# Group-dependent start addresses for the gated values and for w_in in a Fourier filter with a gated feed-forward

## The chip, the cores and the metric

The kernel runs on one core of a Trainium2 chip. The metric is the device time of one execution in microseconds; every number below is in microseconds (us) unless it says ns. The engines are named as in the profile: PE (TensorE, the matmuls), PEld (the loading of the stationary operand of a matmul, the "weights"), DVE (VectorE), ACT (ScalarE), POOL (GpSimd) and SP (SyncE, which issues the DMAs).

## The reference

Input x is 8 batches of 3136 rows by 256 columns. It is filtered along the rows in the Fourier domain, and the result goes through a feed-forward with an inner width of 1024:

```python
X = np.fft.rfft(x, axis=1)
x = np.fft.irfft(X * (filt_r + 1j * filt_i)[None], n=3136, axis=1).astype(np.float32)
h = np.maximum(x @ w_in, 0.0)                       # w_in 256 x 1024
conv = sum(conv_w[k] * shift(h, k - 1) for k in range(3))   # along the rows, per column
gate = 1.0 / (1.0 + np.exp(-conv))
out = (h * gate @ w_out).astype(np.float32)         # w_out 1024 x 256
```

## The kernel before

There are two stages. The forward stage transforms, filters and transforms back with matmuls by table (`first`, `second`, `filt`, `third`), with an intermediate in DRAM between them; w_in and w_out arrive in it as doubles, are turned to float32 by DVE, and are then split into a high and a low part (`convert_weights`: ACT writes the high part, POOL the low part, `hi_act` and `lo_pool`). `wi[0]`, `wi[1]` are the high and the low part of w_in, `wo[0]`, `wo[1]` those of w_out.

The second stage is the feed-forward. It runs over `j` (28 pieces of 896 rows), within that over `f` (8 groups of 128 of the inner width) and within that over `i` (2 halves of 448 rows). A step `m` is one (j, f, i). The order on every engine is written out by hand (`tc.manual_schedule`): in round m PE does `inner` of step m, in some rounds the last part of the inverse transform of the next batch (`last_stage`, 8 matmul instructions on line L216), and `project` of step m - 6. The other engines follow behind: `relu` and `conv` of step m - 1, `gate` of step m - 2, `split_g` of step m - 3.

Every product is made of three matmuls, high by high, high by low, low by high:

- `inner(j, f, i)`: 6 matmuls (lines L177, L178, L179 for each of two halves k of the 256 columns). The stationary operand is 128 columns of `wi[0]` or `wi[1]`, the moving operand 450 columns of `ys[b][0]` or `ys[b][1]`, the high and low part of the filtered rows (`y0`, `y1` below).
- `project(j, f, i)`: for 4 or 3 blocks of 128 rows, 3 matmuls each (lines L475, L476, L477). The stationary operand is 128 columns of the gated values `g0` (high) or `g1` (low), the moving operand 256 columns of `wo[0]` or `wo[1]`.

So the stationary operand of one matmul is read from SBUF while the moving operand of the matmul before it streams, and both reads go to fixed addresses. In the program's layout all of those addresses are the same modulo 256 bytes, whatever the group, the half, the batch and the buffer:

| operand | bytes between its slices | start modulo 256 |
|---|---|---|
| `wi[0]`, `wi[1]` of group f (stationary) | 512 per f, 4096 per k | 160 |
| `y0`, k = 0 and k = 1 (moving) | 1792 per half of rows | 160, 168 |
| `y1`, k = 0 and k = 1 (moving) | 1792 per half of rows | 192, 200 |
| `g0`, `g1` (stationary), four buffers each | 512 per block, 3584 per buffer | 224 |
| `wo[0]`, `wo[1]` of group f (moving) | 1024 per f | 160 |
| `br`, loaded for L216 (stationary) | 512 | 160 |
| `t`, from which `g0` and `g1` are made | 1792 per buffer | 224 |

`br` is what `last_stage` loads as its stationary operand.

Of the kernel before, what the change touches and what calls it, by code (L numbers as in the profile page):

```python
# [10 lines left out]
F32R = mybir.dt.float32r  # L11
# [10 lines left out]
FF = 1024  # L22
KT = D // 128
NF = FF // 128
SUB = 448
NSUB = S // SUB
CH = 2 * SUB
NT = CH // 128


def _k1(g, s):
# [93 lines left out]
def tile_fft_filter_gated_ffn(  # L125
# [19 lines left out]
    def hi_act(dst, src):  # L145
        nc.scalar.activation(dst, src, AF.Copy)  # L146
# [4 lines left out]
    def lo_pool(dst, src, hi):  # L151
        nc.gpsimd.tensor_tensor(out=dst, in0=src, in1=hi.bitcast(F32), op=ALU.subtract)  # L152

    def to_f32(dst, raw, e, m):


        v = nc.vector
        pairs = raw.rearrange("p (n t) -> p n t", t=2)
        low, high = pairs[:, :, 0].bitcast(U32), pairs[:, :, 1]
        v.tensor_scalar(e, high, 3, 0x3FFFFFF8, op0=ALU.logical_shift_left, op1=ALU.bitwise_and)  # L160
        yield
        v.tensor_scalar(m, high, 30, 30, op0=ALU.logical_shift_right, op1=ALU.logical_shift_left)
        yield
        v.tensor_tensor(out=e, in0=e, in1=m, op=ALU.bitwise_or)
        yield
        v.tensor_scalar(m, high, 27, 0xF, op0=ALU.logical_shift_right, op1=ALU.bitwise_and)
        yield
        v.scalar_tensor_tensor(out=dst, in0=m, scalar=7.0, in1=e.bitcast(F32), op0=ALU.is_ge, op1=ALU.mult)
        yield
        v.tensor_scalar(e, dst.bitcast(I32), 23, 23, op0=ALU.logical_shift_right, op1=ALU.logical_shift_left)  # L170
        yield
        v.scalar_tensor_tensor(out=e.bitcast(F32), in0=low, scalar=2.0**-52, in1=e.bitcast(F32), op0=ALU.mult, op1=ALU.mult)
        yield
        nc.gpsimd.tensor_tensor(out=dst, in0=dst, in1=e.bitcast(F32), op=ALU.add)

    def mm3(ps, wh, wl, rh, rl, start=True, stop=True, **kw):
        nc.tensor.matmul(ps, lhsT=wh, rhs=rh, start=start, stop=False, **kw)  # L177
        nc.tensor.matmul(ps, lhsT=wh, rhs=rl, start=False, stop=False, **kw)  # L178
        nc.tensor.matmul(ps, lhsT=wl, rhs=rh, start=False, stop=stop, **kw)  # L179
# [5 lines left out]
    wc = ctx.enter_context(tc.tile_pool(name="wc", bufs=1))  # L185
# [1 line left out]
    cw = wc.tile([128, 3, NF], F32, name="cw")  # L187
    nc.gpsimd.memset(cw[:, 0, 0:1], 0.0)
    nc.scalar.activation(cw[:, 0, 0:1], cw[:, 0, 0:1], AF.Sigmoid)
    wi = [wc.tile([128, KT, FF], F32R, name=f"wi{h}") for h in range(2)]  # L190
    wo = [wc.tile([128, NF, D], F32R, name=f"wo{h}") for h in range(2)]


    ys, yps = {}, []
# [33 lines left out]
    with (  # L228
# [31 lines left out]
        def load_weights(k):  # L260
            raws[k] = raw = cv.tile([128, 2, 512], I32, name="raw")
            for part, src in enumerate((w_in, w_out)):
                nc.sync.dma_start(out=raw[:, part], in_=src[:, 512 * k:512 * k + 512])
# [9 lines left out]
        def convert_weights():  # L273

            for k in range(8):
                raw = raws.pop(k)
                em = cv.tile([128, 2, 512], I32, name="em", bufs=1)
                ws = cv.tile([128, 2, 256], F32, name="ws")
                yield from to_f32(ws.rearrange("p t n -> p (t n)"), raw.rearrange("p t n -> p (t n)"), em[:, 0], em[:, 1])
                yield  # L280
                parts = [[t.rearrange("p a b -> p (a b)")[:, 256 * k:256 * k + 256] for t in w] for w in (wi, wo)]
                for part, (wh, wl) in enumerate(parts):
                    hi_act(wh, ws[:, part])
                yield
                for part, (wh, wl) in enumerate(parts):
                    lo_pool(wl, ws[:, part], wh)
                    yield
                if k < 6:
                    load_weights(k + 2)

        NP = 14
        parts = {}
# [68 lines left out]
        for c in range(1, 4):  # L361
            nc.sync.dma_start(out=s1_sb[:, 4 * c:4 * c + 4], in_=s1[:, 4 * c:4 * c + 4])
            load("x", 0, 2 * c)
            load("x", 0, 2 * c + 1)
        csteps, wsteps = convert_conv(), convert_weights()
        done = NP * B + 8
        NI = max(NP * B + SKEW + 5, done + N2 // 2 + 3)
        with tc.manual_schedule(engines=COMPUTE):
            for i in range(NI):
                f, m = i, i - SKEW  # L370
# [16 lines left out]
                if 12 <= i < 26 and i % 2 == 0:  # L387
                    sl = slice((i - 12) // 2 * 4, (i - 12) // 2 * 4 + 4)
# [31 lines left out]
    wp = ctx.enter_context(tc.tile_pool(name="wp", bufs=2, reuse_waits="tile"))  # L420
    ps_h = ctx.enter_context(tc.tile_pool(name="ps_h", bufs=4, space=bass.MemoryType.PSUM, reuse_waits="tile"))
    ps_o = ctx.enter_context(tc.tile_pool(name="ps_o", bufs=1, space=bass.MemoryType.PSUM, reuse_waits="tile"))

    outv = out.rearrange("b s d -> (b s) d").rearrange("(j t p) d -> j p t d", p=128, t=NT)
    hs, ts, gs, pos = {}, {}, {}, {}
# [4 lines left out]

    def inner(j, f, i):
        ps = ps_h.tile([128, 512], F32, name="ps_h")[:, 0:SUB + 2]
        fs = slice(128 * f, 128 * f + 128)
        b, u = divmod(2 * j + i, NSUB)
        us = slice(u * SUB, u * SUB + SUB + 2)
        for k in range(KT):
            mm3(ps, wi[0][:, k, fs], wi[1][:, k, fs], ys[b][0][:, k, us], ys[b][1][:, k, us], start=k == 0, stop=k == KT - 1)
        hs[j, f, i] = ps

    def relu(j, f, i):  # L440
# [16 lines left out]
    def split_g(j, f, i):  # L457
        t = ts.pop((j, f, i))
        if i == 0:
            gs[j, f] = [wp.tile([128, 2 * SUB], F32R, name=f"g{h}", bufs=4) for h in range(2)]  # L460
        gh, gl = (g[:, i * SUB:i * SUB + SUB] for g in gs[j, f])
        hi_act(gh, t)
        lo_pool(gl, t, gh)

    def project(j, f, i):
        gh, gl = gs[j, f]
        if f == 0 and i == 0:
            pos[j] = [ps_o.tile([128, 512], F32, name=f"po{k}") for k in range(4)], wp.tile([128, NT, D], F32, name="ot")
        po, ot = pos[j]
        tiles = range(4) if i == 0 else range(4, NT)  # L470
        for t in tiles:
# [7 lines left out]
    def evacuate(j, f, i):  # L479
# [4 lines left out]
        for k in (0, 1) if i == 0 else (2, 3):  # L484
            n = min(2, NT - 2 * k)
            o, src = ot[:, 2 * k:2 * k + n].rearrange("p t d -> p (t d)"), po[k][:, 0:n * D]
# [11 lines left out]
    for b in range(1, B):  # L498
        start = ((NSUB * (b - 1) - 1) // 2 + 1) * 16 + (4 if b == 1 else 0)
        stop = NSUB * b // 2 * 16 + NSUB * b % 2  # L500
# [3 lines left out]
    with tc.manual_schedule(engines=COMPUTE):  # L504
        for m in range(NH + PLAG):
            if m + 4 in pieces:
                last_load(*pieces[m + 4])
            if a := at(m):
                inner(*a)
            if m in pieces:  # L510
                last_stage(*pieces[m], ps_h.tile([128, 512], F32, name="ps_h"))
            if a := at(m - PLAG):
                project(*a)
            if a := at(m - 1):
                relu(*a)
                conv(*a)
            if a := at(m - 2):
                gate(*a)
            if a := at(m - 3):
                split_g(*a)  # L520
            if m in pieces:
                last_out(*pieces[m])
            if a := at(m - PLAG):
                evacuate(*a)
# [44 lines left out]
```

## Time and profile before

| | |
|---|---|
| median of 3 runs | 1564.86 (1562.59 to 1569.63) |
| the profiled execution's own time | 1563.82 |
| its span, first to last instruction | 1562.0 |
| PE busy | 1503.0, 96% of the span |
| PEld busy | 1346.7, 86% |
| DVE busy | 1280.6, 82% |
| ACT busy | 1189.7, 76% |
| POOL busy | 697.6, 45% |
| granted PE clock, mean | 0.990 |

The durations that the profile gives for matmuls overlap, since matmuls are pipelined and their ends are modelled. What one matmul costs is therefore read here as the distance from its start to the start of the next one, called its pitch. "x" behind a row counts its instructions.

### The profile page before, as it was taken

What the parts mean: (1) busy time and instruction counts of PE and PEld (TensorE: products, weight loads), DVE (VectorE), ACT (ScalarE), POOL (GpSimd) and SP (SyncE); (2) the same over time, 40 slices, a digit from 0 to 9 for tenths busy, and PEclk for the clock granted to TensorE, in tenths of its full rate; (3) what the DMA queues carried; (4) which work ended last, traced back from release to release, by engine and by line L of the source; (5) the groups of instructions that cost most, each with busy time, mean ns of one, the idle gap of its engine ahead of it and who ended that gap; (6) DMA issues with size and microseconds to landing.
All of it is one profiled execution on the core that took longest, in us unless ns stands there. A gap on an engine that the chain in (4) does not pass through costs nothing.

```text
span 1562.0 us, 26357 instructions
## 1 busy us (share of the span) xinstructions
PE 1503.0 (96%) x9424; PEld 1346.7 (86%) x9424; DVE 1280.6 (82%) x1965; ACT 1189.7 (76%) x2162; POOL 697.6 (45%) x624
## 2 busy tenths in 40 slices
PE   5799989998999999999999999999999999999998
PEld 3466656656999999999999999999999999999998
DVE  0578888888888888888888888888888888888887
ACT  3444444436888888888888888888888888888887
POOL 0356555643444444444444444444444444444444
PEclk9799999999999999999999999999999999999999
DMA  9999999993111011111110111111011110100001
GB/s 306 298 342 350 330 339 343 335 280 105 31 54 48 31 48 48 48 48 48 48 42 28 33 55 48 48 48 48 31 42 48 48 53 25 48 25 25 25 25 48
DMA packets 129397, 166.82 MB, mean 107 GB/s; under 512 B 10906, under 2 KB 87795, under 8 KB 129267
## 3 DMA queue, kind: packets, MB, share of 16 engines
q1 hardware_dynamic: 129267, 165.14, 32.8%
q8 instruction: 75, 1.23, 0.3%
q14 instruction: 55, 0.45, 0.1%
HBM read 88.03 MB, written 77.07 MB: 106 GB/s over the span
## 4 chain that ended last, share of the span: by engine, by line
PE 82%; DMA 12%; DVE 2%; SPq 1%; ACT 1%; issue 1%; POOL 0%; ACTq 0%; POOLq 0%
PE ps_h L178 12%; PE ps_h L179 12%; PE ps_h L177 11%; PE po L475 11%; PE po L477 11%; PE po L476 11%; PE ps_h L216 6%; DMA a<-a_dram 4%; DMA a_dram<-sa 3%; PE pp L328 3%; PE ps L351 2%; PE ps L321 2%; DMA b_dram<-sb 2%; DVE y L149 1%; ACT y L146 1%
## 5 line engine op out<-in xcount | busy, mean ns | idle before, releaser
L152 POOL TENSOR_TENSOR g<-t,g 128x448 fp32r<-128x448 f32 x448 | 517.5, 1155 | 668.2 <-ACT g L146 266.5
L475 PE MATMUL po<-wo,g 128*128 128x256 f32 x1568 | 441.5, 282 | 0.0
L477 PE MATMUL po<-wo,g 128*128 128x256 f32 x1568 | 433.8, 277 | 0.0
L476 PE MATMUL po<-wo,g 128*128 128x256 f32 x1568 | 433.4, 276 | 0.0
L449 DVE SCALAR_TENSOR_TENSOR t<-ps_h,cw,t 128x448 f32<-128x448 f32 x448 | 305.5, 682 | 82.8 <-ACT t L444 71.9
L178 PE MATMUL ps_h<-y,wi 128*128 128x450 f32 x896 | 330.4, 369 | 4.6 <-DVE y L149 4.6
L177 PE MATMUL ps_h<-y,wi 128*128 128x450 f32 x896 | 328.5, 367 | 3.2 <-DVE t L455 1.5
L179 PE MATMUL ps_h<-y,wi 128*128 128x450 f32 x896 | 328.6, 367 | 0.0
L450 DVE SCALAR_TENSOR_TENSOR t<-ps_h,cw,t 128x448 f32<-128x448 f32 x448 | 306.4, 684 | 16.0
L444 ACT ACTIVATE t<-ps_h,cw 128x448 f32<-128x448 f32 x448 | 285.1, 636 | 41.8 <-POOL g L152 0.4
L475 PEld LDWEIGHTS po<-wo,g 128*128 128x128 f32 x1568 | 294.7, 188 | 7.0
L476 PEld LDWEIGHTS po<-wo,g 128*128 128x128 f32 x1568 | 294.3, 188 | 5.7
L477 PEld LDWEIGHTS po<-wo,g 128*128 128x128 f32 x1568 | 294.4, 188 | 0.0
L442 ACT ACTIVATE ps_h<-ps_h 128x450 f32<-128x450 f32 x448 | 251.7, 562 | 31.8 <-PE ps_h L179 27.2
L455 DVE TENSOR_TENSOR t<-ps_h,t 128x448 f32<-128x448 f32 x448 | 275.1, 614 | 0.1
L454 ACT ACTIVATE t<-t 128x448 f32<-128x448 f32 x448 | 255.0, 569 | 12.1 <-DVE t L450 10.9
L146 ACT ACTIVATE g<-t 128x448 fp32r<-128x448 f32 x448 | 254.4, 568 | 0.2 <-DVE t L455 0.2
L344 POOL TENSOR_TENSOR z<-u,v 120x512 f32<-120x512 f32 x112 | 156.8, 1400 | 172.3 <-DVE v L342 162.9
L309 ACT ACTIVATE sb<-ps 112x512 f32<-112x512 f32 x112 | 66.8, 597 | 159.2 <-DMA b_dram<-sb 87.9
L179 PEld LDWEIGHTS ps_h<-y,wi 128*128 128x128 f32 x896 | 168.3, 188 | 13.9
L178 PEld LDWEIGHTS ps_h<-y,wi 128*128 128x128 f32 x896 | 168.3, 188 | 13.6 <-DVE y L149 6.8
L177 PEld LDWEIGHTS ps_h<-y,wi 128*128 128x128 f32 x896 | 169.9, 190 | 11.5 <-DVE t L455 2.6
(51 smaller groups left out, 1474.0 us busy)
## 6 DMA issues: line engine op xcount, KB each, us to landing
x<-in_x SPq DMA_DIRECT2D x112, 224.0 KB, 4.8
a_dram<-sa SPq DMA_DIRECT2D x112, 224.0 KB, 4.5
a<-a_dram SPq DMA_DIRECT2D x112, 224.0 KB, 4.7
b_dram<-sb SPq DMA_DIRECT2D x112, 224.0 KB, 4.5
br<-b_dram SPq DMA_DIRECT2D x112, 224.0 KB, 2.6
out<-ot SPq DMA_DIRECT2D x27, 896.0 KB, 4.1
raw<-in_w_in SPq DMA_DIRECT2D x8, 256.0 KB, 4.6
raw<-in_w_out SPq DMA_DIRECT2D x8, 256.0 KB, 5.6
```

The source lines that it names most:

```text
L146: nc.scalar.activation(dst, src, AF.Copy)
L152: nc.gpsimd.tensor_tensor(out=dst, in0=src, in1=hi.bitcast(F32), op=ALU.subtract)
L177: nc.tensor.matmul(ps, lhsT=wh, rhs=rh, start=start, stop=False, **kw)
L178: nc.tensor.matmul(ps, lhsT=wh, rhs=rl, start=False, stop=False, **kw)
L179: nc.tensor.matmul(ps, lhsT=wl, rhs=rh, start=False, stop=stop, **kw)
L444: nc.scalar.activation(t, h[:, 1:SUB + 1], AF.Copy, scale=cw[:, 1, f:f + 1])
L449: nc.vector.scalar_tensor_tensor(out=t, in0=h[:, 0:SUB], scalar=cw[:, 0, f:f + 1], in1=t, op0=ALU.mult, op1=ALU.add)
L450: nc.vector.scalar_tensor_tensor(out=t, in0=h[:, 2:SUB + 2], scalar=cw[:, 2, f:f + 1], in1=t, op0=ALU.mult, op1=ALU.add)
L455: nc.vector.tensor_mul(t, h[:, 1:SUB + 1], t)
L475: nc.tensor.matmul(o, lhsT=gh[:, sl], rhs=wo[0][:, f], start=first, stop=False, skip_group_check=True)
L476: nc.tensor.matmul(o, lhsT=gh[:, sl], rhs=wo[1][:, f], start=False, stop=False, skip_group_check=True)
L477: nc.tensor.matmul(o, lhsT=gl[:, sl], rhs=wo[0][:, f], start=False, stop=last, skip_group_check=True)
```

## The change

Each group's 128 columns of `wi` get a row of 136 elements instead of 128, so that group f starts 544 bytes behind group f - 1 instead of 512: its start modulo 256 is now 160 + 32 f. Each buffer of `g0` and `g1` is 32 elements longer, and group f uses it from element 4 f on, so 16 f bytes further in; a buffer is 3712 bytes instead of 3584. Everything allocated behind `wi` moves up by 512 or 1024 bytes. The starts modulo 256 are then:

| f | 0 | 1 | 2 | 3 | 4 | 5 | 6 | 7 |
|---|---|---|---|---|---|---|---|---|
| `wi[0]`, `wi[1]` | 160 | 192 | 224 | 0 | 32 | 64 | 96 | 128 |
| `g0`, `g1` | 224 | 112 | 0 | 144 | 32 | 176 | 64 | 208 |

`y0`, `y1`, `wo`, `t` and `br` keep theirs. Every engine issues the same instructions in the same order as before. Two things beside the addresses differ: the 8 copies by ACT and the 8 subtractions by POOL that write `wi` go over 128 x 2 x 128 elements instead of 128 x 256, and three of POOL's first writes of `g1` wait for other DMAs of the forward stage than before, because `g1` now lies over other old tiles.

```diff
+WROW = 136
+GSTEP = 4
...
-    wi = [wc.tile([128, KT, FF], F32R, name=f"wi{h}") for h in range(2)]
+    wi = [wc.tile([128, KT, NF, WROW], F32R, name=f"wi{h}")[:, :, :, 0:128] for h in range(2)]
...
-                parts = [[t.rearrange("p a b -> p (a b)")[:, 256 * k:256 * k + 256] for t in w] for w in (wi, wo)]
+                wv = ws.rearrange("p t (f n) -> p t f n", n=128)
+                parts = [[t[:, k // 4, 2 * (k % 4):2 * (k % 4) + 2] for t in wi],
+                         [t[:, k].rearrange("p (f n) -> p f n", n=128) for t in wo]]
                 for part, (wh, wl) in enumerate(parts):
-                    hi_act(wh, ws[:, part])
+                    hi_act(wh, wv[:, part])
                 yield
                 for part, (wh, wl) in enumerate(parts):
-                    lo_pool(wl, ws[:, part], wh)
+                    lo_pool(wl, wv[:, part], wh)
...
-        fs = slice(128 * f, 128 * f + 128)
...
-            mm3(ps, wi[0][:, k, fs], wi[1][:, k, fs], ys[b][0][:, k, us], ys[b][1][:, k, us], start=k == 0, stop=k == KT - 1)
+            mm3(ps, wi[0][:, k, f], wi[1][:, k, f], ys[b][0][:, k, us], ys[b][1][:, k, us], start=k == 0, stop=k == KT - 1)
...
         if i == 0:
-            gs[j, f] = [wp.tile([128, 2 * SUB], F32R, name=f"g{h}", bufs=4) for h in range(2)]
+            sl = slice(GSTEP * f, GSTEP * f + 2 * SUB)
+            gs[j, f] = [wp.tile([128, 2 * SUB + 32], F32R, name=f"g{h}", bufs=4)[:, sl] for h in range(2)]
```

## The prediction

> **What bounds the kernel now.** I read the page first: the busy times, the 40 slices and the chain of work that ended last.
>
> ```profile
> span 1562.0 us, 26357 instructions
> ...
> PE 1503.0 (96%) x9424; PEld 1346.7 (86%) x9424; DVE 1280.6 (82%) x1965; ACT 1189.7 (76%) x2162; POOL 697.6 (45%) x624
> ...
> PE   5799989998999999999999999999999999999998
> ...
> PEclk9799999999999999999999999999999999999999
> DMA  9999999993111011111110111111011110100001
> ...
> PE 82%; DMA 12%; DVE 2%; SPq 1%; ACT 1%; issue 1%; POOL 0%; ACTq 0%; POOLq 0%
> ```
>
> The slices show two stages. In the first quarter the DMA engines are at nine tenths, behind it they are nearly idle and PE is full. PE carries 82% of the chain. The view by stretches gives both stages in numbers; its columns are PE, PEld, DVE, ACT and POOL busy, then the granted clock, the DMA share and GB/s:
>
> ```profile
> 0.00:385.00 385.00, 334.54 (x1284) 224.49 (x1284) 282.35 (x424) 172.87 (x284) 180.59 (x150) 0.96 0.94 307
> 395.00:1562.00 1167.00, 1158.84 (x8079) 1113.47 (x8077) 989.25 (x1529) 1007.46 (x1861) 511.44 (x466) 1.00 0.13 41
> ```
>
> The change touches the second stage, 1167 us of the span. PE is busy there in 1158.8 of it, at a clock of 1.00. ACT, the next engine, is busy for 1007.5, so it leaves 159 us of room. The forward stage is bound by DMA (share 0.94).
>
> Next I read the timeline of PE alone where no inverse transform is mixed in. These are the first matmul of a group f = 0 (1473.32), its first L475 (1474.54), its second half (1475.90, then L475 at 1477.13), and the first matmuls of groups 1 to 5; the second fence has groups 5 and 6 of the next piece, 14 groups after the first:
>
> ```profile
> 1473.32 0.37 PE L177 MATMUL ps_h<-y,wi 128*128 128x450 f32 x1
> ...
> 1474.54 0.28 PE L475 MATMUL po<-wo,g 128*128 128x256 f32 x1
> ...
> 1475.90 0.37 PE L177 MATMUL ps_h<-y,wi 128*128 128x450 f32 x1
> ...
> 1477.13 0.28 PE L475 MATMUL po<-wo,g 128*128 128x256 f32 x1
> ...
> 1478.15 0.37 PE L177 MATMUL ps_h<-y,wi 128*128 128x450 f32 x1
> ...
> 1482.98 0.37 PE L177 MATMUL ps_h<-y,wi 128*128 128x450 f32 x1
> ...
> 1487.82 0.37 PE L177 MATMUL ps_h<-y,wi 128*128 128x450 f32 x1
> ...
> 1492.65 0.37 PE L177 MATMUL ps_h<-y,wi 128*128 128x450 f32 x1
> ...
> 1497.48 0.37 PE L177 MATMUL ps_h<-y,wi 128*128 128x450 f32 x1
> ```
>
> ```profile
> 1536.15 0.37 PE L177 MATMUL ps_h<-y,wi 128*128 128x450 f32 x1
> ...
> 1540.98 0.37 PE L177 MATMUL ps_h<-y,wi 128*128 128x450 f32 x1
> ```
>
> Every group takes 4.83 or 4.84: (1540.98 - 1473.32) / 14 = 4.833. A group is 12 matmuls of 450 columns and 21 of 256. The 21 take (1475.90 - 1474.54) + (1478.15 - 1477.13) = 2.38, a pitch of 113.3 ns; the 12 take the other 2.453, a pitch of 204.4 ns. The groups differ in `wi`, in `wo`, in the buffer of `g`, in the rows of `y`, and in what DVE, ACT and POOL do beside them, and none of that moves the group by 10 ns. So PE runs at a pitch of its own; it doesn't wait, and where 256 bytes or more lie between two addresses the pitch doesn't follow them.
>
> The chain between 900 and 903 us shows the pitches one by one (start, us, what):
>
> ```profile
> 900.54 0.20 PE ps_h L179
> 900.74 0.12 PE po L475
> ...
> 901.76 0.20 PE ps_h L177
> 901.97 0.20 PE ps_h L178
> 902.17 0.20 PE ps_h L179
> 902.37 0.20 PE ps_h L177
> 902.57 0.21 PE ps_h L178
> 902.78 0.21 PE ps_h L179
> 902.99 0.88 PE ps_h L216 x8
> ```
>
> L179 is followed by an L475 at 900.54, by an L177 at 902.17 and by L216 at 902.78, so beside it `g` (start 224 modulo 256), `wi` (160) or `br` (160) is being loaded. The moving operand starts at 160 (k = 0) or 168. The pitch is 0.20, 0.20 and 0.21. Of the residues below 256 these are all that the trace has for the long matmuls, and they are worth at most 10 ns.
>
> **The change, part by part.** The stage is 224 groups of 4.833 us, with 224 x 12 = 2688 long matmuls (550 us) and 224 x 21 = 4704 short ones (533 us). A change of the mean pitch by 1 ns is therefore worth 2.7 us in the long and 4.7 us in the short ones, and both go to the end undiluted, since PE is the path.
>
> *The start of `wi`.* It is read for the 2688 loads beside the long matmuls and the last short one. The load and the moving stream pass over addresses at different speeds: 512 bytes in at most the 188 ns of a load (the first row of the next fence), 1800 bytes in 204.4 ns, so 2.7 and 8.8 bytes per ns. One stream overtakes the other by some 1100 bytes in one load. A start moved by 32 f, at most 224 bytes, shifts the moment at which two reads meet in the same place, but hardly how often they meet. That is why I take 0 here. The bounds: L177 to L179 differ by 10 ns at most between the residues that occur, so the mean over eight residues should move by less than half of that, 5 ns; 2688 x 5 = 13 us either way.
>
> ```profile
> L475 PEld LDWEIGHTS po<-wo,g x1568: 187/188/192, 386.8 to 1557.3; 128*128 128x128 f32 x196
> ...
> L146 ACT ACTIVATE wi<-ws x8: 407/408/418, 85.2 to 303.8; 128x256 fp32r<-128x256 f32 x8
> L152 POOL TENSOR_TENSOR wi<-ws,wi x8: 722/728/735, 88.2 to 307.0; 128x256 fp32r<-128x256 f32 x8
> ```
>
> *The start of `g`.* It is read for the 4704 loads of L475 to L477. A load lasts 188 ns and they follow each other at 113.3 ns, so here a longer load would have little to hide behind. By the same overtaking I take 0. All starts stay multiples of 16 bytes. The bounds are the rivals below. The writes of `g` by ACT and POOL keep their number and size; if they became dearer, ACT's 159 us of room over 448 steps is 0.36 us per step.
>
> *One rule against one row.* A long matmul costs 204.4 / 450 = 0.454 ns per column, a short one 113.3 / 256 = 0.443, so the long one is dearer than its columns by 204.4 - 450 x 0.443 = 5.2 ns, and no wait of the trace explains that. If a meeting of reads is behind it, 2688 x 5.2 = 14 us could go. The Trainium skill ("SBUF — State Buffer", section "Who interferes with whom") gives TensorE two independent read ports, one for the moving operand and one for the weight load, and says that it never waits on anyone; by that the two streams can't meet at all and the change is worth exactly nothing. The trace can't decide between a collision and a fixed cost of the long form, because the residues never change in it.
>
> *The writes of `wi`.* 8 copies of 408 ns on ACT and 8 subtractions of 728 ns on POOL now have rows of 128 elements. They lie between 85 and 307 us, where the DMA share is 0.94 and ACT is busy for 173 of 385 us. Even if all 16 took twice as long (9 us together) they would be under that cover, and without it they would cost these 9 us. I take 0.
>
> *POOL's changed waits.* Three of the first writes of `g1` wait for other loads and stores of the forward stage than before. Two of them are these, and what ended their wait was ACT's write of `g0`:
>
> ```profile
> 390.92 1.16 POOL L152 TENSOR_TENSOR g<-t,g 128x448 fp32r<-128x448 f32 x1 [0.93 <-ACT g L146]
> ...
> 396.37 1.15 POOL L152 TENSOR_TENSOR g<-t,g 128x448 fp32r<-128x448 f32 x1 [2.06 <-ACT g L146]
> ```
>
> The other loads and stores were issued earlier still, and PE needs a `g` three rounds after it is split. The price is 0; the upper bound is one round of PE, 4.833 / 2 = 2.4 us.
>
> The sum is 0 on the profiled execution's 1563.82, whose span is 1562.0; the median of the runs is 1.04 higher. I predict the median, 1564.9.
>
> **The rivals.** Half a percent, about what a measurement of this kernel can tell from no change, is 7.8 us.
>
> *Faster: the streams do meet, and fixed residues make it bad.* For it: the 5.2 ns that a long matmul costs over its columns, and that all residues are locked now, so that a bad one hits every group. Against it: three different sources loaded beside L179 give the same pitch to 10 ns. The price: the long ones go to 199.2 ns (14 us), and the short ones go to what L216 needs, which loads 128 columns as well and is bound by it with 112 moving ones, 0.88 / 8 = 110 ns (3.3 x 4704 = 15.5 us). Group 0 keeps its addresses, so 7/8 of 29.5: 25.8 us, 1539. By the Trainium skill's gap of N / 2.4 + 2.5 ns ("TensorE: Matmul & The Clock Gate", section "Back-to-back issue gap"), which no row here reaches, 190.0 and 109.2 ns would be free of stalls, and 7/8 of 58 us would give an estimate of 1514.
>
> *Slower: a load pays for where it starts.* The odd groups' `g` now starts at 16 modulo 32, which no load did before. If a load from there needs one more access, it goes to the pitch of the short matmuls, whose loads are back to back. For it: the only starts in the trace that differ by a fraction of 32 bytes, those of `y` with k = 1, stand beside the 0.21 of L178. Against it: the L177 with the same shift stays at 0.20. The price is between 0 and the 10 ns between these rows; halfway, 5 ns on half of 4704 loads is 11.8 us, 1576.7, and the full 10 ns give 1588. It decides from 7.8 us / 2352 = 3.3 ns per load on.
>
> *Another engine becomes the bound.* Only if PE gained more than ACT's 159 us; no case here reaches that.
>
> **How the numbers follow.** No change: 0.72, from a group time that is equal to 10 ns over all groups, and from the overtaking of the streams. Faster: 0.15, for a stall that no wait explains and that locked residues could hide. Slower: 0.13, for starts that were never seen. The time is that of no change, 1564.9; its own range is 1557 to 1573. The range for 8 in 10 goes down to the long matmuls at the rate of the short ones (1564.9 - 14 = 1551) and up to the slower rival at 5 ns (1577).
>
> **What would show it.** The groups of the last four pieces have one length each, so the timeline of PE tells every start apart. If I am right, all eight last 4.83 still. If the faster rival holds, group 0 stays at 4.83 and others fall below, by up to 0.13 us (12 x 5.2 + 21 x 3.3 ns). If the slower one holds, the odd groups take longer than the even ones by 21 x 5 ns, 0.1 us. If long and short matmuls change apart, `wi` and `g` are told apart by the spans from L177 to L475 and from L475 to L177. I would be wrong if the number of meetings depended on the start after all, for example if a stall locked the two streams into step; then a group's length would follow f without regard to odd or even.

## The result, and the profile after

The changed kernel is 1.3% slower: 1586.74 us in the median (1581.59 to 1588.79, 4 runs) against 1565.39 for the kernel before beside it (1562.59 to 1569.63, 4 runs). The ratio is 1.0129, with a 95% interval from 1.0096 to 1.0163. No change was forecast, 1564.9 in a range of 1551 to 1577; the time lies above the range.

The lines of the page that answer to those shown of before, and the second stage in the view by stretches:

```profile
span 1579.8 us, 26357 instructions
...
PE 1522.1 (96%) x9424; PEld 1366.0 (86%) x9424; DVE 1281.7 (81%) x1965; ACT 1190.8 (75%) x2162; POOL 696.9 (44%) x624
...
PE 83%; DMA 10%; DVE 3%; SPq 2%; issue 1%; ACT 1%; POOL 0%; ACTq 0%; POOLq 0%
```

```profile
413.00:1580.00 1167.00, 1158.72 (x7938) 1113.31 (x7936) 973.18 (x1504) 990.49 (x1828) 502.67 (x459) 1.00 0.13 41
```

Nothing of this shows a cause. PE is as full as before (1158.7 of 1167 us) at the same clock, waits for nobody, and the other engines are as busy as before; PE only takes 19 us longer for the same 9424 matmuls (1522.1 against 1503.0). In the same 1167 us it gets through 7938 matmuls instead of 8079. The cause is in the pitch. Here is the timeline of PE at the first matmuls of groups 0 to 5 of piece 26 (L177 to L179 are now L179 to L181, L475 to L477 are L479 to L481), with the short matmuls of one step in group 3:

```profile
1489.26 0.37 PE L179 MATMUL ps_h<-y,wi 128*128 128x450 f32 x1
...
1494.19 0.36 PE L179 MATMUL ps_h<-y,wi 128*128 128x450 f32 x1
...
1499.15 0.36 PE L179 MATMUL ps_h<-y,wi 128*128 128x450 f32 x1
...
1504.06 0.37 PE L179 MATMUL ps_h<-y,wi 128*128 128x450 f32 x1
...
1505.29 0.28 PE L479 MATMUL po<-wo,g 128*128 128x256 f32 x1
...
1506.66 0.37 PE L179 MATMUL ps_h<-y,wi 128*128 128x450 f32 x1
...
1508.92 0.36 PE L179 MATMUL ps_h<-y,wi 128*128 128x450 f32 x1
...
1513.84 0.37 PE L179 MATMUL ps_h<-y,wi 128*128 128x450 f32 x1
```

The groups take 4.93, 4.96, 4.91, 4.86 and 4.92, where each took 4.83 before. `project` trails by six steps, so the stretch that begins with the long matmuls of group 3 holds the short ones of group 0, whose `g` kept its start: it is the shortest, and its 12 short matmuls take 1506.66 - 1505.29 = 1.37 (114 ns each). The stretch of group 7 holds the short matmuls of group 4:

```profile
1524.97 0.28 PE L479 MATMUL po<-wo,g 128*128 128x256 f32 x1
1525.09 0.28 PE L480 MATMUL po<-wo,g 128*128 128x256 f32 x1
...
1526.41 0.36 PE L179 MATMUL ps_h<-y,wi 128*128 128x450 f32 x1
```

Those 12 take 1.44, 120 ns each. Each group's length is the same in pieces 25 and 26 to within 1 ns, so this is not noise but a fixed pattern of each group.

To compare many kernels, the following numbers are worked out from the starts of all matmuls of each trace: the pitch is the mean distance from one start to the next (distances over 300 ns in the long and over 160 ns in the short matmuls, which stand beside a wait or a first one, and long ones before an inverse transform are left out), and the group is the mean length of the 16 groups of pieces 25 and 26. The last column is 224 times what a group is longer than before.

| kernel | long, ns | short, ns | group, ns | 224 groups, us |
|---|---|---|---|---|
| before | 204.6 | 113.5 | 4833 | 0 |
| changed | 205.0 | 117.8 | 4932 | +22.0 |
| g alone | 204.6 | 117.7 | 4925 | +20.5 |
| wi alone | 204.9 | 115.0 | 4871 | +8.4 |
| g by 16 f, buffers alike | 205.3 | 118.2 | 4943 | +24.6 |
| the same, and wo by 16 f | 204.9 | 115.1 | 4875 | +9.3 |
| wo alone by 32 f | 204.7 | 117.8 | 4930 | +21.7 |
| g by 4 f | 205.1 | 117.5 | 4936 | +23.0 |
| halves of y alike, wi by 32 f | 205.0 | 116.3 | 4903 | +15.7 |
| all distances 64 | 206.1 | 117.4 | 4953 | +26.9 |
| the same, and wi by 32 f | 205.0 | 117.1 | 4924 | +20.4 |
| halves of y alike | 203.0 | 115.0 | 4860 | +6.0 |
| g by 24 everywhere | 204.6 | 115.8 | 4887 | +12.0 |
| wi by 64 everywhere | 203.3 | 114.2 | 4833 | 0.0 |

The last column holds for groups without an inverse transform (`last_stage`) and takes all 224 to be like them. Measured over the whole stage, from the start of its first long matmul to that of its last step, the profiled execution takes 1194.7 in place of 1174.7, so 20.0 longer; its forward stage was 2.5 shorter and its span 17.8 longer. The medians differ by 21.4. The short matmuls alone account for 4704 x 4.3 = 20 us.

### The profile page after: what moved, and what is told of

Its sections match the earlier page's. It is cut to its first block, busy times and chain, and to the rows that moved or that the text cites. A ratio compares the mean times of both kernels' runs of the same rounds, so it can differ in the third digit from the quotient of the medians.

```text
span 1579.8 us, 26357 instructions
## 1 busy us (share of the span) xinstructions
PE 1522.1 (96%) x9424; PEld 1366.0 (86%) x9424; DVE 1281.7 (81%) x1965; ACT 1190.8 (75%) x2162; POOL 696.9 (44%) x624
## 4 chain that ended last, share of the span: by engine, by line
PE 83%; DMA 10%; DVE 3%; SPq 2%; issue 1%; ACT 1%; POOL 0%; ACTq 0%; POOLq 0%
PE ps_h L180 12%; PE po L479 12%; PE ps_h L179 12%; PE po L480 12%; PE ps_h L181 12%; PE po L481 11%; DMA a<-a_dram 6%; PE ps_h L218 5%; PE pp L332 3%; PE ps L355 2%; DMA a_dram<-sa 2%; PE ps L325 2%; DMA b_dram<-sb 1%; DVE y L151 1%; DVE v L345 1%
## 5 line engine op out<-in xcount | busy, mean ns | idle before, releaser
L479 PE MATMUL po<-wo,g 128*128 128x256 f32 x1568 | 447.5, 285 | 0.0
L480 PE MATMUL po<-wo,g 128*128 128x256 f32 x1568 | 439.0, 280 | 0.0
L481 PE MATMUL po<-wo,g 128*128 128x256 f32 x1568 | 438.9, 280 | 0.0
L179 PE MATMUL ps_h<-y,wi 128*128 128x450 f32 x896 | 331.3, 370 | 3.2 <-DVE t L458 1.5
L181 PE MATMUL ps_h<-y,wi 128*128 128x450 f32 x896 | 328.5, 367 | 0.0
L479 PEld LDWEIGHTS po<-wo,g 128*128 128x128 f32 x1568 | 295.1, 188 | 5.7
L480 PEld LDWEIGHTS po<-wo,g 128*128 128x128 f32 x1568 | 295.0, 188 | 5.2
L481 PEld LDWEIGHTS po<-wo,g 128*128 128x128 f32 x1568 | 295.0, 188 | 0.0
L181 PEld LDWEIGHTS ps_h<-y,wi 128*128 128x128 f32 x896 | 169.0, 189 | 15.7
L179 PEld LDWEIGHTS ps_h<-y,wi 128*128 128x128 f32 x896 | 169.0, 189 | 12.4 <-DVE t L458 2.6
```

What stands on the lines that cost most here:

```text
L479: nc.tensor.matmul(o, lhsT=gh[:, sl], rhs=wo[0][:, f], start=first, stop=False, skip_group_check=True)
L480: nc.tensor.matmul(o, lhsT=gh[:, sl], rhs=wo[1][:, f], start=False, stop=False, skip_group_check=True)
L481: nc.tensor.matmul(o, lhsT=gl[:, sl], rhs=wo[0][:, f], start=False, stop=last, skip_group_check=True)
```

## The experiments

"Distance" is the start of the stationary operand minus that of the moving one beside it, modulo 256 bytes. Theory A: the distance decides. Rival B: the start of the load itself decides. Rival C: it is the rows of wi. The diffs are against the changed kernel and show what is particular to a run. Where wi is as before, WROW is 128; where g is as before, GSTEP is 0 and its buffers are not padded.

**The change on g alone.** wi keeps 512 bytes per group.

```diff
-WROW = 136
+WROW = 128
```

> The change on g alone: g starts 16 f bytes further in and its buffers are 3712 bytes apart; wi stays at 512 bytes per group. In the changed kernel the short matmuls went from a mean pitch of 113.5 to 117.8 ns and the long ones from 204.7 to 205.3. Theory A (the load of a stationary operand and the moving operand that streams beside it meet in SBUF, and how often depends on the distance between their starts): the short matmuls stay at 117 to 119 ns, so about 4704 x 4.3 = 20 us over the kernel before, 1585. Rival B (a load pays for where it starts itself, whatever streams beside it): the same here, 1585. Rival C (the loss is that of the new rows of wi): at most 2 us over before, 1567.

1583.68 us, ratio 1.0116 (1.0101 to 1.0131). The short matmuls take 113.3 ns in group 0 and 117.3 to 119.5 in the others; the long ones stay at 204.6. So g carries nearly all of the loss. Rival C falls.

**The change on wi alone.**

```diff
-GSTEP = 4
+GSTEP = 0
-... [128, 2 * SUB + 32] ...
+... [128, 2 * SUB] ...
```

> The change on wi alone: rows of 544 bytes, g as before. Theories A and B: the long matmuls change by the 0.5 ns that they changed by in the changed kernel, 2688 x 0.5 = 1.4 us, about 1567. Rival C: all of the loss, 1585.

1573.99 us, ratio 1.0057 (1.0040 to 1.0074): dearer than both theories said. The long matmuls changed as expected (204.9), the loss is in the short ones, 115.0 against 113.5 ns, though neither g nor wo was moved: 4704 x 1.5 = 7 us. Their first three or four after the long ones are at 115 to 123 ns and the rest at 113 in most steps; in the first half of group 2, where no inverse transform stands before them, all twelve stay at about 118. The losses do not add up: 18.1 us for g alone and 8.4 for wi alone, 21.4 for both. This was the first sign that a short matmul depends on more than its own two addresses.

**g by 16 f with all buffers alike, and the same with wo moved along.** The last two lines are in the second kernel alone:

```diff
-WROW = 136
+WROW = 128
-... [128, 2 * SUB + 32] ...
+... [128, 2 * SUB + 64] ...
-    wo = [wc.tile([128, NF, D], F32R, ...
+    wo = [wc.tile([128, NF * (D + 4) + 32], F32R, name=f"wo{h}")[:, 0:NF * (D + 4)].rearrange("p (f d) -> p f d", f=NF)[:, :, 0:D] for h in range(2)]
```

> g starts 16 f bytes further in, with buffers 3840 bytes apart, so that all buffers start alike modulo 256 and group f starts at 224 + 16 f; wi as before. Theories A and B: group f = 0 keeps 113.3 ns in its short matmuls, most other groups lie at 116 to 119 ns. If it was the half step of 128 bytes between buffers that cost, and not the 16 f, all groups lie at 113 to 114 ns.

> As the run before it, and wo of group f also starts 16 f bytes further in, so that the stationary g and the moving wo keep their distance of 64 bytes modulo 256 while both leave their old starts. Theory A: the short matmuls are back at 113 to 114 ns in all groups, 1565 to 1567. Rival B: they stay as in the run before, 116 to 119 ns in most groups, about 1583.

g alone: 1588.60, ratio 1.0147 (1.0126 to 1.0167). With wo along: 1572.61, ratio 1.0047 (1.0031 to 1.0063). The 12 short matmuls of the first half of group 4 in the first kernel, and in the second:

```profile
1531.53 0.28 PE L479 MATMUL po<-wo,g 128*128 128x256 f32 x1
...
1532.96 0.36 PE L179 MATMUL ps_h<-y,wi 128*128 128x450 f32 x1
```

```profile
1518.67 0.28 PE L479 MATMUL po<-wo,g 128*128 128x256 f32 x1
...
1520.03 0.37 PE L179 MATMUL ps_h<-y,wi 128*128 128x450 f32 x1
```

1.43 against 1.36, the time of before. g starts at 32 modulo 256 in both; only the distance to wo differs, 128 and 64. So the start of the load itself is not what costs. The mean came back to 115.1, not to 113.5: many steps have slow first matmuls, and two, the first half of group 2 and the second half of group 4, stay at about 118 ns throughout, at the same distance of 64.

**wo alone, by 32 f.**

```diff
-    wo = [wc.tile([128, NF, D], F32R, ...
+    wo = [wc.tile([128, NF * (D + 8)], F32R, name=f"wo{h}").rearrange("p (f d) -> p f d", f=NF)[:, :, 0:D] for h in range(2)]
```

> g and wi as in the kernel before; wo of group f starts 32 f bytes further in. So it is the moving operand that moves, and the distance from wo to g goes round the circle modulo 256: 64, 32, 0, 224, 192, 160, 128, 96 for f = 0 to 7. Theory A (the distance decides): group 0 keeps 113.3 ns, groups 5 and 6 (160, 128) lie at 118 to 120 as the same distances did with g moved, group 7 (96) at 117 to 118; 32, 0, 224 and 192 are new and show whether another distance is as good as 64. Rival B (the loaded operand's own start decides): g didn't move, so all groups at 113 to 114 ns and about 1566. Theory A without another good distance: 7/8 x 4704 x 5 = 20 us over before, 1586.

1586.75 us, ratio 1.0137 (1.0104 to 1.0170). Group 0 has 113.8 ns, all others 117.1 to 119.7. g was not moved, so rival B is out, and of the eight distances in steps of 32 bytes none is as good as 64. wo is written in the forward stage alone, so the writes of ACT and POOL into g, which were where they are in the kernel before, are not the cause either.

**g by 4 f.**

```diff
-WROW = 136
+WROW = 128
-GSTEP = 4
+GSTEP = 1
-... [128, 2 * SUB + 32] ...
+... [128, 2 * SUB + 64] ...
```

> g of group f starts 4 f bytes further in (distances 64, 68, 72, 76, 80, 84, 88, 92; all buffers alike), wi and wo as in the kernel before. If pieces of 16 bytes are what meets, groups 0 to 3 stay near 113 to 114 ns and groups 4 to 7 near the 118.6 that the distance 80 had. If the exact distance counts, groups 1 to 3 are at 116 to 119 as well. In the first case about 4704 x 2.6 = 12 us over before, 1578, in the second 1586.

1585.03 us, ratio 1.0126 (1.0092 to 1.0160). Groups 0 to 7 have 114.8, 118.2, 118.1, 118.0, 118.6, 119.4, 115.2 and 118.0 ns. 4 bytes off are as dear as 16, so it is the exact distance and not the 16-byte piece; and group 6, at 88, comes back to 113 ns within its steps.

The mean of group 3, at 76, hides two patterns. Its second half has nine short matmuls, here in piece 21 and in piece 25:

```profile
1320.16 0.28 PE L479 MATMUL po<-wo,g 128*128 128x256 f32 x1
...
1321.18 0.37 PE L179 MATMUL ps_h<-y,wi 128*128 128x450 f32 x1
```

```profile
1487.69 0.28 PE L479 MATMUL po<-wo,g 128*128 128x256 f32 x1
...
1488.77 0.37 PE L179 MATMUL ps_h<-y,wi 128*128 128x450 f32 x1
```

They take 1.02 and 1.08, 113 and 120 ns each, with the same g buffers, the same wo and all starts alike modulo 256. The difference is what came before: in all ten pieces with an inverse transform in the half before, this half is at 113, and in all ten with none in either half it is at 120. So one kernel has both patterns at one distance, and history decides between them.

**The halves of y alike, and wi by 32 f.**

```diff
-            ys[b] = [yps[b % 2].tile([128, KT, S + 2], F32R, name=f"y{h}") for h in range(2)]
+            ys[b] = [yps[b % 2].tile([128, KT * 3200 + 8], F32R, name=f"y{h}")[:, 0:KT * 3200].rearrange("p (k s) -> p k s", k=KT) for h in range(2)]
```

> g and wo as in the kernel before; each half k of y gets a row of 3200 elements, so that both halves start alike modulo 256 (160 for y0, 192 for y1) where the second stood 8 bytes off; wi of group f starts 32 f bytes further in. It asks whether the long matmuls have a distance at which they lose the 5 ns that they cost over their columns. Theory A with a good distance among the eight: one or two groups' long matmuls fall to 199 to 201 ns, the others stay at 203 to 207. If the long form's surplus is a fixed cost, no group falls below 203 in the mean of its six. The time is 1565 to 1575 either way, since entering and leaving the short matmuls costs some ns as with wi moved alone (1574).

1580.36 us, ratio 1.0103 (1.0074 to 1.0133), above what was expected. Single long matmuls fall to 197 to 199 ns in groups 0, 2, 4 and 6 (and others rise to 207 to 212), so the surplus is not the same for each long matmul. But by the sign set beforehand, the mean of six, no group fell below 203 (they are at about 203 to 208), and the short matmuls, at the old distance of 64, stay at 117 to 118 ns through whole steps, those of groups 0 and 2 among them.

**All distances at 64, and the same with wi by 32 f.** Padding puts every moving operand of the feed-forward at 160 and every stationary one at 224 modulo 256; y gets the rows of 3200 elements and 64 elements more, of which the even batches skip 48; wi has WROW = 128 in the first kernel and 136 in the second, and g is as before in both.

```diff
+    wc.tile([128, 16], F32, name="pad_m2")
     m2_sb = wc.tile([112, N1], F32, name="m2_sb")
...
+    wc.tile([128, 48], F32, name="pad_wo")
     wo = [wc.tile([128, NF, D], F32R, ...
...
+    wp.tile([128, 16], F32, name="pad_t", bufs=1)
```

> No start differs from group to group; instead every moving operand of the feed-forward (y0 and y1 with both halves k, wo) starts at 160 modulo 256 and every stationary one (wi, g, br) at 224, so that all of them have the distance of 64 at which the short matmuls of the kernel before ran at 113.3 ns. Theory A (the distance decides, for the long matmuls too): the long ones fall from 204.7 to 198 to 201 ns, 2688 x 4 to 7 = 10 to 18 us, and the short ones keep 113.3, so 1547 to 1555. If the long form's surplus is a fixed cost, nothing moves: 1565. If the long form needs another distance than the short one, the long ones are at 203 to 208 and the time at 1562 to 1575.

> As the run before it, but wi of group f starts 32 f bytes further in, so that the distance from y to wi goes round the circle: 64, 96, 128, 160, 192, 224, 0, 32 for f = 0 to 7, alike for all six long matmuls of a step. Theory A: the groups' long matmuls differ, at least one distance gives 198 to 201 ns, most give 203 to 208. If the surplus is a fixed cost, all groups are within 1 ns of 204.7.

The first: 1587.12 us, ratio 1.0125 (1.0108 to 1.0142). The second, one run: 1584.59 beside a median of 1566.42 before. Theory A as it stood fell here. In the first kernel every step without an inverse transform is alike, and slow. The rows of one are its first long, its first short and the next step's first long matmul, and the next group's start:

```profile
1495.06 0.37 PE L179 MATMUL ps_h<-y,wi 128*128 128x450 f32 x1
...
1496.30 0.28 PE L483 MATMUL po<-wo,g 128*128 128x256 f32 x1
...
1497.71 0.37 PE L179 MATMUL ps_h<-y,wi 128*128 128x450 f32 x1
...
1500.02 0.37 PE L179 MATMUL ps_h<-y,wi 128*128 128x450 f32 x1
```

The 6 long ones take 1.24 (206 ns each), the 12 short ones 1.41 (117.6 ns), though g and wo start modulo 256 as they did before, when the 12 took 1.36. So the distance counts (113 was reached at 64, 76 and 88 and at no other that was tried), but it is not enough: at 64 the short matmuls have two patterns that last through a step, 113.3 and 117.6. Which one they take depends on what stands before them. In the same kernel, a step in which the inverse transform stands between the long and the short matmuls falls to 113 after the first five. These are the first, the sixth and the seventh of its 12, and the next long one:

```profile
1416.15 0.36 PE L483 MATMUL po<-wo,g 128*128 128x256 f32 x1
...
1416.83 0.28 PE L485 MATMUL po<-wo,g 128*128 128x256 f32 x1
1416.94 0.28 PE L483 MATMUL po<-wo,g 128*128 128x256 f32 x1
...
1417.62 0.39 PE L179 MATMUL ps_h<-y,wi 128*128 128x450 f32 x1
```

The last seven take 0.79, 113 ns each, with g and wo at the same starts modulo 256 as in the slow steps. It is most of the reason why the stage is only 19.8 us longer here and not 26.9. In the second kernel the long matmuls' means by group go from about 203 to 208, so their distance counts as well, but no distance gives 198 to 201 in all six.

**The halves of y alike, and nothing else.** wi, g and wo are those of the kernel before.

```diff
-            ys[b] = [yps[b % 2].tile([128, KT, S + 2], ...
+            ys[b] = [yps[b % 2].tile([128, KT * 3200 + 8], ...
```

> The kernel before with one thing changed, and nothing from group to group: the second half k of y starts where the first does modulo 256 (160 for y0, 192 for y1) instead of 8 bytes behind. wi, g and wo start as before, so the short matmuls keep their distance of 64. If that distance alone decides (theory A as it stood), the short matmuls stay at 113.3 ns and the time at 1565. If the short matmuls have two lasting patterns at this distance, 113.3 and 117.6, and the long ones before them decide which one they enter (theory A2, formed after the run with all distances at 64), they can be at 117.6 throughout, 4704 x 4.3 = 20 us over before, about 1585.

1570.11 us, ratio 1.0032 (1.0017 to 1.0046), less than A2 allowed and more than A. All steps have one and the same pattern, here the first five short matmuls of one and the end of the step:

```profile
1479.78 0.28 PE L479 MATMUL po<-wo,g 128*128 128x256 f32 x1
1479.90 0.29 PE L480 MATMUL po<-wo,g 128*128 128x256 f32 x1
1480.03 0.28 PE L481 MATMUL po<-wo,g 128*128 128x256 f32 x1
1480.15 0.28 PE L479 MATMUL po<-wo,g 128*128 128x256 f32 x1
1480.26 0.28 PE L480 MATMUL po<-wo,g 128*128 128x256 f32 x1
...
1481.17 0.37 PE L179 MATMUL ps_h<-y,wi 128*128 128x450 f32 x1
```

The first three have pitches of 0.12, 0.13 and 0.12, and then it is 0.11 as before. 8 bytes in the second half of y, which no short matmul reads, cost each step some 20 ns on the way into its short matmuls (119, 124 and 119 ns in place of 113 each), and give back 10 ns in the long ones (203.0). So the long matmuls decide how the short ones are entered. This run does not show them holding the short ones in the slow pattern; the kernel with all distances at 64 does, where the same short matmuls leave it once the inverse transform stands between.

**g by 24 everywhere.**

```diff
-            sl = slice(GSTEP * f, GSTEP * f + 2 * SUB)
+            sl = slice(6, 6 + 2 * SUB)
```

> g starts 24 bytes further in for all groups alike (distance 88 to wo, at which group 6 of the run in steps of 4 bytes fell to 113 ns), all else as in the kernel before. It asks whether a constant start other than before's holds the short pattern. If 88 is as good a distance as 64, all groups stay at 113 to 114 ns and the time at 1565 to 1568; if group 6 was a chance of its neighbours, 117 to 119 ns and 1585. A loss here would also show that a constant shift costs as much as one that differs from group to group.

1576.32 us, ratio 1.0065 (1.0045 to 1.0086), between the two cases. The first short matmul, the seventh, and the end of the step:

```profile
1486.97 0.28 PE L479 MATMUL po<-wo,g 128*128 128x256 f32 x1
...
1487.68 0.28 PE L479 MATMUL po<-wo,g 128*128 128x256 f32 x1
...
1488.36 0.37 PE L179 MATMUL ps_h<-y,wi 128*128 128x450 f32 x1
```

Six matmuls in 0.71 (118 ns), then six in 0.68 (113 ns). At the distance 88 the short matmuls come to the good pattern too, but only after six. A start that is the same in all groups thus costs as well; the spread from group to group is not what hurts.

**wi by 64 everywhere.**

```diff
+    wc.tile([128, 16], F32, name="pad_wi")
     wi = [wc.tile(...
+    wc.tile([128, 48], F32, name="pad_wo")
     wo = [wc.tile(...
```

> wi starts 64 bytes later for all groups alike (224 modulo 256, so at distance 64 from y0), all else as in the kernel before. With wi moved alone, group 2, which had this distance, had steps of 1218 ns for their six long matmuls (before: 1227) and in one of its halves kept the short ones at 113. If that pattern can hold in every group, 448 x 9 ns = 4 us less, 1561; if the short ones enter at 117.6 as in that group's other half, 10 to 20 us more, 1575 to 1585.

1565.09 us, ratio 0.9994 (0.9983 to 1.0005): no difference. The 6 long matmuls of a step, then its 12 short ones:

```profile
1476.18 0.36 PE L179 MATMUL ps_h<-y,wi 128*128 128x450 f32 x1
...
1477.40 0.28 PE L481 MATMUL po<-wo,g 128*128 128x256 f32 x1
...
1478.77 0.36 PE L179 MATMUL ps_h<-y,wi 128*128 128x450 f32 x1
```

1.22 and 1.37. By the starts to the ns, the first long matmul falls from 205 to 198 ns and the six to 1219 from 1228; the first two short ones rise to 117 and 116, and the group is 4833 again. Gain and loss cancel. No version that was tried beats the kernel before.

**Half the stream, half the load.** These four leave out a part of the small products, so their times are not to be compared as such. In the first pair L480 and L481 stream 128 of the 256 columns of wo; in the second pair they load 64 of the 128 columns of g. Each ran once: 1568.00, 1563.48, 1564.53 and 1582.85 us, in the order below, beside 1568.04 before. In each pair the first kernel has the addresses of before, the second has g by 16 f with buffers alike.

```diff
-            nc.tensor.matmul(o, lhsT=gh[:, sl], rhs=wo[1][:, f], ...
+            nc.tensor.matmul(o[:, 0:128], lhsT=gh[:, sl], rhs=wo[1][:, f, 0:128], ...           # half the stream
+            nc.tensor.matmul(o[0:64], lhsT=gh[:, 128 * t:128 * t + 64], rhs=wo[1][:, f], ...    # half the load
```

> Addresses as in the kernel before; L476 and L477 stream only 128 of the 256 columns of wo (the small parts of half the output are left out), their loads stay whole. If the load of 128 columns sets the short pitch, the two stay near 113 ns each and the time at 1565. If the stream of 256 columns sets it, they fall to the floor of the load, which must then lie below 113.

> As the run before it with g of group f starting 16 f bytes further in (alike buffers). If two reads that meet cost the time, half the stream leaves half of the meetings, and L476 and L477 fall from 118 to 119 ns towards the 113 of the run before it, while L475, whose stream is whole, stays dear. If the start of the load itself costs (rival B), L476 and L477 stay at 117 to 120.

> Addresses as in the kernel before; L476 and L477 load only 64 of the 128 columns of g (the small parts of half the rows are left out), their streams stay whole. If the load sets the short pitch, the matmul beside which a half load runs (L475, L476) falls from 113 to about 109 or less, the pace of a stream of 256 columns alone; if the stream sets it, nothing moves.

> As the run before it with g of group f starting 16 f bytes further in (alike buffers). If the dear pattern is a load that is held up, half a load has room and L475 and L476 fall to the same pitch as in the run before it, whatever f. If it is the stream that is held up, they stay above it by about half of the 5 ns that whole loads cost.

Half the stream: groups of 4847 ns with the addresses of before and 4846 with g moved, so with half the stream the place of g costs nothing in the sum. Three matmuls of the first kernel:

```profile
1508.28 0.33 PE L479 MATMUL po<-wo,g 128*128 128x256 f32 x1
1508.45 0.22 PE L480 MATMUL po<-wo,g 128*128 128x128 f32 x1
1508.51 0.28 PE L481 MATMUL po<-wo,g 128*128 128x128 f32 x1
1508.62 0.34 PE L479 MATMUL po<-wo,g 128*128 128x256 f32 x1
```

Three loads of 128 columns take 0.34 here, 113 ns each, as before: the loads keep the pace though the streams are half. The expectation that L476 and L477 would stay at 113 each was wrong in its form (L480 to L481 is 0.06); the three together tell it.

Half the load: groups of 4833 ns with the addresses of before, and 4918 with g moved, 19 us over 224 groups. The load of 64 columns in the first kernel, and a step's 12 short matmuls in the first and, for group 4, in the second:

```profile
L480 PEld LDWEIGHTS po<-wo,g x1568: 133/134/138, 385.8 to 1558.2; 128*64 128x64 f32 x196
```

```profile
1504.25 0.28 PE L479 MATMUL po<-wo,g 128*128 128x256 f32 x1
...
1505.61 0.37 PE L179 MATMUL ps_h<-y,wi 128*128 128x450 f32 x1
```

```profile
1526.44 0.28 PE L479 MATMUL po<-wo,g 128*128 128x256 f32 x1
...
1527.84 0.38 PE L179 MATMUL ps_h<-y,wi 128*128 128x450 f32 x1
```

A load of 64 columns is 54 ns shorter (134 against 188), and the pitch stays at 113 ns: the stream of 256 columns needs the 113 ns as well. With g moved the 12 take 1.40 although the loads now have room, and two thirds of the columns loaded leave 85 of the 110 ns that a group was longer with whole loads. The two beside which half a load runs are dear themselves: by the starts, L479 takes 116 to 118 ns and L480 117 to 118 in groups 1 to 7. So what is held up here is the stream, since the load has room. That the load beside it holds it up is concluded from the distance between the two; no run streams without loads.

## Why the prediction was wrong, point by point

*What bounds the kernel* was right: PE at a pitch of its own, no wait, and each ns in the short matmuls worth 4.7 us. It is why a place in memory could reach the end undiluted.

*The step that failed* is the one on which both zeros rest, "shifts the moment at which two reads meet in the same place, but hardly how often they meet", and after it "By the same overtaking I take 0" for g. For the short matmuls that term was 0 and measured 4704 x 4.3 = 20 us. The reasoning treated one load beside one stream as if it began at random. What the runs show is a pattern that repeats and that depends on what came before: at 113.3 ns at the distance of 64 when the short matmuls are entered as in the kernel before, at 113 after some matmuls at 88 and in some steps at 76, and at 117 to 120 ns at every other distance that was tried. The kernel before stood at 64 in every step, and its short matmuls came behind the long ones without any slow first ones. The prediction's last sentence named such a lock ("if a stall locked the two streams into step") as a way to be wrong, but it gave it neither a price nor a chance of its own.

*The evidence was read too far.* "Every group takes 4.83" was taken to say that addresses don't matter. It says that nothing matters that is the same modulo 256 bytes in all groups. The text named that limit ("where 256 bytes or more lie between two addresses") and then gave 0.72 to no change, though the trace held no second distance between g and wo at all. Here the equal groups were a locked pattern, and 4 bytes were enough to break it.

*The 10 ns bound.* The three rows of L179 with g, wi and br beside it were right in their size, and for the long matmuls the bound of 5 ns held: their mean moved by 0.4 ns. It was not a bound for the short ones, where load and stream both need 113 ns and neither has room.

*The start of wi* was taken as 0 with a bound of 13 us. Alone it costs 8.4 us, but in a term that the prediction did not have: 7 us of it are the short matmuls that come after the long ones.

*The slower rival* had the sign, the place (the short matmuls) and at its full price of 10 ns nearly the time (1588), with 0.13. That the time is near is chance, for its mechanism is refuted: odd groups are not dearer than even ones (group 4, at 0 modulo 32, has 119.1 ns), and moving wo instead of g costs the same.

*The rule of two independent ports* in the Trainium skill ("SBUF — State Buffer", section "Who interferes with whom"), by which the change is worth nothing, does not hold for these matmuls: the same loads and streams take 113 or 118 ns by the distance between them. The faster rival's estimate by the Trainium skill's gap formula ("TensorE: Matmul & The Clock Gate", section "Back-to-back issue gap"), 190.0 and 109.2 ns, which the page gives as the gap of an isolated matmul, was not reached either: no kernel's mean was below 203.0 for the long matmuls, or below 113.5 for the short ones with whole loads and streams.

*The writes of wi, and POOL's changed waits* were 0, as taken: the 8 copies take 412 ns instead of 408, the 8 subtractions 730 instead of 728, under the same cover, and the first long matmul starts at 371.2 us, where it was 373.7.

*What would show it* was the right view with one slip: the stretch of group 0 does not hold group 0's short matmuls, but those of group 5 of the piece before, and it was the stretch of group 3 that stayed shortest (4.86).

What stays open: whether and where in the memory the two reads meet, why 64, 76 and 88 can be good and 68 or 96 are not (the three lie 12 bytes apart, and 52 and 100 were not tried), and by what the long matmuls of the kernel with all distances at 64 hold the short ones at 117.6. The runs show that distance and entry decide, not how.

## What to carry to other kernels

In this kernel PE is full, waits for nobody, and its groups are equal to the ns, and yet its pitch depends on where the stationary and the moving operand lie to each other, modulo 256 bytes. Padding a tensor, or giving a buffer another size, cost it 1.3% with the same instructions in the same order. Such a loss is read from the starts of the matmuls, group by group, since the busy shares did not show it (PE 96% in both). A constant in a trace tells nothing of what was never varied in it; such a quantity deserves a run, or a wide range.

## What the runs showed of the hardware that I had not expected

- The pitch of matmuls with 256 moving columns is 113.3 ns at a distance of 64 bytes between load and stream, comes to 113 at 88 and at times at 76, and is 117 to 120 ns at the others that were tried; 4 bytes are enough to change it.
- At one and the same distance two patterns last (113.3 and 117.6 ns at 64, 113 and 120 at 76), in one kernel, and the matmuls before decide which; 8 bytes in an operand of the long matmuls add some 20 ns to the short ones behind them.
- Loads of 128 columns beside half streams, and streams of 256 columns beside half loads, each go at 113 ns, so in this form neither has room to hide a delay.
- Single long matmuls ran at 197 to 199 ns where their mean is 204.6, so by an estimate from these an arrangement with up to 2688 x 6.6 = 18 us less may exist; no arrangement that was tried had such a pitch in all six of a step, nor together with 113.3 in all short ones.
